# Other landing counts and other drawn due times for a planner that orders one core's instructions at build time

## The chip, the cores and the metric

The kernel runs on one core of one Trainium2 chip. Its time is the device time of one execution in microseconds (us); the median of several executions counts. A core has a tensor engine (PE, with its weight loads shown apart as PEld), a vector engine (DVE), a scalar engine (ACT), a general engine (POOL) and a queue engine (SP). Each runs its own list of instructions strictly in the order in which it was written, and waits on semaphores where an instruction needs another engine's result or a landed transfer. Transfers (DMAs) are issued from SP and POOL here. A DMA issued from POOL can add to what lies at its destination.

## The reference

```python
def _attn_ref(q, k, v, g_norm):                   # q, k, v: (8, 8, 576, 64) float32
    kv = np.einsum('bhsd,bhse->bhde', k, v)
    out = np.einsum('bhsd,bhde->bhse', q, kv)
    rms = np.sqrt(np.mean(out * out, axis=-1, keepdims=True) + 1e-06)
    return out / rms * g_norm

def _moe_ref(x, domain_probs, w1, w2):            # x: (4608, 512); 4 experts, 512 -> 1024 -> 512
    p = domain_probs / (domain_probs.sum(-1, keepdims=True) + 1e-09)
    for e in range(4):
        h = np.maximum(x @ w1[e], 0.0)
        out += p[:, e:e + 1] * (h @ w2[e])
```

The first function's output, with heads beside each other, is the second one's x. All is float32.

## The kernel before

**Tiles and stages.** The 4608 rows of x are worked on in 9 chunks of 512 (eight batches, and one chunk of what is left over of each). There are 36 steps, one for each expert and chunk: steps 0 to 8 are expert 0, and so on. Attention for the next chunk runs beside the steps of expert 0; its results are written to HBM and loaded again for experts 1 to 3. At the end of an expert (steps 8, 17 and 26) the next expert's weights are loaded.

**Products.** The matrix products use a Strassen-Winograd scheme, in parts in two levels: seven products in place of eight, of sums and differences of blocks. PE multiplies; ACT and DVE copy and add PE's results out of its banks; DVE and POOL form the sums and differences (L549), either engine where the planner gives it a choice. Each product is issued by `halves_of` (L526) as matmuls on half the array; one product of the inner level is eight of them.

**Weights.** For experts 1 to 3 a difference that needs a block of weights from HBM is made by `subtract_from`: ACT copies a tile with its sign changed (L622), then POOL issues a DMA that adds the HBM block onto it (L628): an *adding weight transfer*. Plain weight loads go through `load` on SP (L555).

**Output.** A chunk's output is collected in `big` buffers. Expert 0 writes it out plainly on SP (L1592); experts 1 to 3 add it onto what lies in HBM, by DMAs from POOL (L1590): *adding output writes*. The very last chunk loads what is there, adds and writes plainly.

**The order.** Nothing is ordered at run time. The program first lists all operations (`plan.add`), each with a key (its place in the sequence of steps), the engines that may run it with a cost on each, the buffers that it reads and writes, and for a DMA its size and `lands`, the least time counted from issue to landing. `Plan.prepare` gives each operation a due time (`base`): from the PE work ahead of its key, pulled forward along its dependences. `Plan.run` then plays the program through: each time that an engine is free, it takes among the operations that are ready the one with the earliest due time (SP takes the first ready one by key), gives it a buffer slot, and writes down the order. `Plan.begin` sets when a DMA's result counts as landed. The instructions are then emitted in that order. So a different landing count or due time moves no work; it changes which operation stands before which, which of DVE and POOL runs a sum, and which buffer slot a result gets.

**Drawn due times.** `Plan.layout` goes step by step. For each step, `deal` looks up a number in the table DEALS and shifts the due times of the operations of that step and the next by noise drawn from that number (`noise`, a hash, the same in each build), with one of three widths for PE operations and one of three others for the rest. A step without an entry has no noise.

Of the kernel before, what the change touches and what calls it, by code (L numbers as in the profile page):

```python
# [41 lines left out]
class Plan:  # L42
# [18 lines left out]
    FORMS = 9.0  # L61
    STEP, LATE = 44.0, 30.0
    SLOW = 6.8
    SPREADS = 1.0, 2.0, 4.0
    SPREADS_PE = 0.0, 0.5, 1.5
    RATE, RATE_POOL, OPEN = 260.0, 130.0, 36.0
    FIRST = "SP",
    DEALS = {
        -2: 8, -1: 32, 0: 171, 1: 147, 2: 82, 3: 196, 4: 105, 5: 75, 6: 79, 7: 39, 8: 54, 9: 73, 10: 115,
        11: 84, 12: 12, 13: 6, 14: 6, 16: 1, 17: 3, 18: 10, 19: 11, 20: 2, 21: 1, 22: 4, 23: 4, 25: 5, 26:  # L70
        8, 27: 6, 33: 3, 34: 4
    }
    SHARED, AHEAD, INORDER = ("big",), 0.3, ("xf",)

# [90 lines left out]
            self.steps.setdefault(math.floor(op.key), []).append(op)  # L165

    @staticmethod
    def noise(*key):

        def mix(x):  # L170
            x = (x ^ x >> 16) * 0x7feb352d & 0xffffffff
            x = (x ^ x >> 15) * 0x846ca68b & 0xffffffff
            return x ^ x >> 16

        n, step, i = key
        x = mix(n * 2654435761 + (step + 8) * 40503 & 0xffffffff)
        x = mix(x + i * 2246822519 & 0xffffffff)
        y = mix(x + 1 & 0xffffffff)
        total = float(x & 0xffff) + float(x >> 16) + float(y & 0xffff) + float(y >> 16)
        return total / 65536.0 * 1.7320508 - 3.4641016  # L180

    def deal(self, step, n):

        k = len(self.SPREADS)
        wide = self.SPREADS[n % k] if n else 0.0
        wide_pe = self.SPREADS_PE[n // k % len(self.SPREADS_PE)] if n else 0.0
        for op in self.steps[step] + self.steps.get(step + 1, []):
            z = wide_pe if "PE" in op.cost else wide
            op.due = op.base + (z * self.noise(n, step, op.n) if z else 0.0)

    def layout(self, *how):

        self.prepare(*how)
        for step in sorted(self.steps):
            self.deal(step, self.DEALS.get(step, 0))
            assert self.run(step + 1)
        self.run(math.inf)
        assert not self.left
        self.length = max(o.end for o in self.order)
        return self.order  # L200
# [130 lines left out]
    def begin(self, op, eng):  # L331
        t, wake, free = self.t, self.wake, self.free
        op.start, op.eng = t, eng
        if eng == "SP":
            self.busy[eng] = t + op.cost[eng]
            self.bus = max(self.bus, t + 1.5) + op.kb / (215.0 if t < self.OPEN else self.RATE)
            op.end = self.bus + 0.5
            if t >= self.OPEN:
                op.end = max(op.end, t + op.lands)
            self.lanes = self.lanes[1:] + [op.end]  # L340
        else:
            op.end = t + op.cost[eng]
            self.busy[eng] = op.end - (self.OVERLAP[eng] if t >= self.OPEN else 0.0)
            if op.kb:
                self.bus_pool = max(self.bus_pool, op.end + 2.0) + op.kb / self.RATE_POOL
                op.end = max(op.end + op.lands, self.bus_pool)
        if eng == "PE":
            self.worked += op.cost[eng]
        if op.port:
            self.port, self.held = op.end, eng  # L350
            heapq.heappush(wake, op.end + self.TURN["DVE"])
            heapq.heappush(wake, op.end + self.TURN["POOL"])
            heapq.heappush(wake, op.end)
        for b in op.outs:
            if b.kind is not None and b.slot is None:
                free[b.kind].sort()
                b.slot = free[b.kind].pop(next(
                    (i for i, f in enumerate(free[b.kind])
                     if self.written.get((b.kind, f[1]), 0) >= op.wants), 0) if op.wants else 0)[1]
                b.ap = self.slots[b.kind][b.slot]  # L360
        if eng == "PE":
            for b in op.outs:
                self.written[b.kind, b.slot] = op.wide.get(b, op.marks[1] if op.marks else 0)
        for held in list(self.waiting.values()) + list(self.first.values()):
            held.pop(op, None)
        for o in self.after[op]:
            self.missing[o] -= 1
            if not self.missing[o]:
                self.arm(o)
        for b in op.bufs:  # L370
            b.left -= 1
            if b.left == 0 and b.kind is not None:
                early = t < self.OPEN
                end = max(
                    o.end + (0.2 if early else self.AFTER_PE if o.eng == "PE" else self.FREED)
                    for o in [op] + b.readers + b.writers)
                free[b.kind].append((end, b.slot))
                self.live[b.kind] -= 1
                self.ended[b.kind] = max(end, self.ended.get(b.kind, 0.0))
                for rule in [r for r in self.later if not any(self.live.get(k) for k in r[0])]:  # L380
                    self.later.remove(rule)
                    end = max(self.ended[k] for k in rule[0])
                    for ap in rule[2]:
                        free.setdefault(rule[1], []).append((end, len(self.slots[rule[1]])))
                        self.slots[rule[1]].append(ap)
                    heapq.heappush(wake, end)
        heapq.heappush(wake, self.busy[eng])
        if t < self.OPEN:
            heapq.heappush(wake, op.end + 0.06)
            heapq.heappush(wake, op.end + 0.2)  # L390
        if op.kb:
            heapq.heappush(wake, op.end + self.LANDED)
        else:
            for more in (0.0, self.AFTER_PE) if eng == "PE" else (
                    self.SAME, self.TO_PE, self.TO_POOL, self.OTHER):
                heapq.heappush(wake, op.end + more)
        self.order.append(op)
        self.left -= 1
# [3 lines left out]
def kernel(  # L402
# [147 lines left out]
            reads=reads, writes=writes, port=True, after=after,  # L550
        )

    def load(key, buf, dst, src, kb, reads=(), also=(), lands=4.0, issue=0.55):
        plan.add(
            key, {"SP": issue}, lambda eng: nc.sync.dma_start(out=dst(), in_=src), reads=reads,  # L555
            parts=[buf] + list(also), kb=kb, lands=lands,
        )
# [52 lines left out]
    def w1_src(e, dh, uh):  # L610
        rows = moe_w1[e][dh * 2 * P:(dh + 1) * 2 * P, uh * HF:(uh + 1) * HF]
        return rows.rearrange("(kt p) f -> p kt f", p=P)

    def w2_src(e, uh, dh):
        rows = moe_w2[e][uh * HF:(uh + 1) * HF, dh * HN:(dh + 1) * HN]
        return rows.rearrange("(kt p) d -> p kt d", p=P)

    def subtract_from(key, to, view, a, src, reads, writes):

        plan.add(  # L620
            key, act(2 * NT),
            lambda eng: nc.scalar.activation(  # L622
                out=to.ap[:], in_=a.ap[:], func=ACT.Copy, scale=-1.0),
            reads=reads, writes=[to],
        )
        plan.add(
            key, {"POOL": 1.3},
            lambda eng: nc.gpsimd.dma_start(out=view(to.ap), in_=src, accum_op=ALU.add),  # L628
            reads=[to], writes=writes, kb=512, lands=6.0,
        )  # L630

    def weights_1(e, key, step, need):

        f = {n: Buf("big", f"w1_{e}_{n}") for n in (1, 2, 21, 4, 5, 6, 7, 3)}
        corner = {}
        w1corner[e] = {}
        for i, (n, dh, uh) in enumerate(((1, 0, 0), (2, 1, 0), (21, 0, 1), (4, 1, 1))):
            corner[n] = Buf(None, f"w1c_{e}_{n}")
            w1corner[e][uh, dh] = f[n], corner[n]
            load(  # L640
                key + i * step if e or i else -2.75, f[n],
                lambda n=n: f[n].ap[:].rearrange("p (k u) -> p k u", k=2),
                w1_src(e, dh, uh), 512 if e else 300, also=[corner[n]], lands=6.0,
            )

        def form(k_, o, a, b, op):
# [45 lines left out]
    def weights_2(e, key, step, deep):  # L692

        f = {n: Buf("big", f"w2_{e}_{n}") for n in (1, 12, 2, 3, 5, 6, 7, 4)}
        corner = w2corner[e] = {}
        for i, (n, uh, dh) in enumerate(((1, 0, 0), (2, 1, 0), (12, 0, 1), (3, 1, 1))):
            corner[n] = Buf(None, f"w2c_{e}_{n}")
            load(
                key + i * step, f[n],
                lambda n=n: f[n].ap[:].rearrange("p (k d) -> p k d", k=4),  # L700
                w2_src(e, uh, dh), 512 if e else 330, also=[corner[n]], lands=6.0,
            )

        def form(k_, o, a, b, op):
# [816 lines left out]
    def result(s, e, c, base):  # L1521
# [60 lines left out]
        def send(key, i):  # L1582
# [4 lines left out]
            def fn(eng):  # L1587
# [6 lines left out]
            plan.add(  # L1594
                key, {"POOL": 1.0 * len(where)} if e and not again else {"SP": 0.55 * len(where)},
                fn, reads=[part[i, 0], part[i, 1]] + ([was] if was else []), writes=[now], kb=256,
                lands=5.6 if e and not again else 4.5,
                holds=[acc[i // 2]],
            )

# [309 lines left out]
    with tc.manual_schedule(engines={ENG.PE, ENG.DVE, ENG.Activation, ENG.Pool, ENG.SP}):  # L1910
# [7 lines left out]
        wide = {}  # L1918
# [42 lines left out]
```

## Time and profile before

| | us |
|---|---|
| median of 3 executions | 1648.17 |
| lowest, highest | 1646.45, 1650.07 |
| the profiled execution's own time | 1651.69 |
| its span, first to last instruction | 1649.9 |
| PE busy in it | 1632.6 |
| DVE busy | 1316.6 |
| ACT busy | 972.8 |
| POOL busy | 620.5 |

The trace comes from one execution, the profiled one. In the rows below, `L526` is line 526 of the kernel above; `u`, `db` and `ab` are PE's banks, `big`, `xf`, `small`, `snap`, `w1y`, `w2y` and `kv` are tiles in the core's memory, `in_moe_w_dram` are the weights in HBM and `out_dram` the output. A chain of waits is read from its end back: each row is what the next one had waited for. SPq is SP issuing a transfer, and a row "DMA a<-b" lasts from its issue to its landing. In a view by windows the columns are the window, its length, then for each engine the busy time and the number of instructions, then the granted clock of PE as a share of the full one, the DMA engines' busy share and GB/s.

### The profile page before, as it was taken

What the parts mean: (1) busy time and instruction counts of PE and PEld (TensorE: products, weight loads), DVE (VectorE), ACT (ScalarE), POOL (GpSimd) and SP (SyncE); (2) the same over time, 40 slices, a digit from 0 to 9 for tenths busy, and PEclk for the clock granted to TensorE, in tenths of its full rate; (3) what the DMA queues carried; (4) which work ended last, traced back from release to release, by engine and by line L of the source; (5) the groups of instructions that cost most, each with busy time, mean ns of one, the idle gap of its engine ahead of it and who ended that gap; (6) DMA issues with size and microseconds to landing.
All of it is one profiled execution on the core that took longest, in us unless ns stands there. A gap on an engine that the chain in (4) does not pass through costs nothing.

```text
span 1649.9 us, 66218 instructions
## 1 busy us (share of the span) xinstructions
PE 1632.6 (99%) x28724; PEld 1554.8 (94%) x28724; DVE 1316.6 (80%) x2188; ACT 972.8 (59%) x2462; POOL 620.5 (38%) x641
## 2 busy tenths in 40 slices
PE   9999999999999999999999999999999999999998
PEld 6688789888999999999999999999999999999997
DVE  5777887878888878788887898777898887778776
ACT  3455554655656666666656666655666566666653
POOL 4132323232433453443344443333344444442333
PEclk9999999999999999999999999999999999999999
DMA  9977886654764435444566444444578444444432
GB/s 230 215 172 206 228 227 174 152 194 175 219 170 130 117 92 155 117 112 109 168 158 167 115 106 119 114 117 113 135 186 187 117 117 117 107 115 116 117 104 53
DMA packets 225597, 240.97 MB, mean 146 GB/s; under 512 B 100890, under 2 KB 165274, under 8 KB 225306
## 3 DMA queue, kind: packets, MB, share of 16 engines
q1 hardware_dynamic: 201690, 199.96, 40.0%
q0 software_dynamic: 23616, 36.78, 14.8%
q8 instruction: 225, 3.69, 0.9%
q14 instruction: 66, 0.54, 0.1%
HBM read 162.21 MB, written 74.47 MB: 143 GB/s over the span
## 4 chain that ended last, share of the span: by engine, by line
PE 92%; DMA 4%; SPq 2%; DVE 1%; issue 1%; ACT 0%; POOL 0%; DVEq 0%; POOLq 0%; ACTq 0%
PE u L526 45%; PE db L526 29%; PE ab L526 15%; DMA out_dram<-big 1%; SPq L555 1%; PE ab L1077 1%; DMA big<-in_moe_w_dram 1%; DMA kv<-in_v_dram 1%; PE ab L1102 1%; DVE big L549 0%; PE ab L1144 0%; DMA big<-roots 0%; PE db L1102 0%; PE ab L1906 0%; PE u L890 0%
## 5 line engine op out<-in xcount | busy, mean ns | idle before, releaser
L549 DVE TENSOR_TENSOR big<-big,big 128x1024 f32<-128x1024 f32 (+1 forms) x539 | 502.0, 946 | 44.8 <-ACT big L1381 18.0
L526 PE MATMUL u<-xf,big 128*64 128x128 f32 x6496 | 476.0, 273 | 0.3
L526 PE MATMUL db<-big,big 128*64 128x128 f32 (+1 forms) x5552 | 425.7, 290 | 1.5 <-ACT big L1745 0.9
L526 PE MATMUL u<-xf,w1y 128*64 128x128 f32 x5304 | 396.5, 273 | 3.8 <-ACT u L1417 2.4
L526 PEld LDWEIGHTS u<-xf,big 128*64 128x64 f32 x6496 | 382.4, 137 | 5.1 <-ACT snap L1417 1.4
L526 PEld LDWEIGHTS db<-big,big 128*64 128x64 f32 x5552 | 332.1, 137 | 28.9 <-ACT big L1745 1.4
L526 PEld LDWEIGHTS u<-xf,w1y 128*64 128x64 f32 x5304 | 314.1, 137 | 8.1 <-ACT u L1417 2.6
L1425 DVE TENSOR_TENSOR big<-u,snap 128x256 f32<-128x256 f32 x448 | 188.3, 421 | 121.2 <-PE u L526 83.7
L1417 ACT ACTIVATE snap<-u 128x256 f32<-128x256 f32 x490 | 187.9, 384 | 148.7 <-PE u L526 130.3
L549 POOL TENSOR_TENSOR big<-big,big 128x256 f32<-128x256 f32 (+1 forms) x145 | 152.7, 1055 | 219.2 <-DVE big L549 111.3
L1417 ACT ACTIVATE big<-u 128x256 f32<-128x256 f32 x448 | 171.1, 385 | 86.9 <-PE u L526 68.0
L549 POOL TENSOR_TENSOR big<-big 128x512 f32<-128x512 f32 (+1 forms) x89 | 107.3, 1207 | 250.7 <-DVE big L549 115.6
L1745 ACT ACTIVATE snap<-db 128x256 f32<-128x256 f32 (+1 forms) x256 | 90.4, 353 | 122.8 <-PE db L526 100.7
L1381 ACT ACTIVATE big<-big 128x1024 f32<-128x1024 f32 x127 | 133.7, 1054 | 12.3 <-DVE big L549 11.2
L1753 DVE TENSOR_TENSOR big<-ab,snap 128x256 f32<-128x256 f32 x174 | 73.2, 421 | 64.4 <-ACT snap L1745 42.6
L1590 POOL DMA_DIRECT2D out_dram<-big x122 | 106.7, 1233 | 31.9 <-ACT big L1566 24.2
L1417 ACT ACTIVATE u<-u 128x256 f32<-128x256 f32 x245 | 90.8, 371 | 37.6 <-PE u L526 25.1
L549 DVE TENSOR_TENSOR big<-big 128x512 f32<-128x512 f32 (+1 forms) x145 | 109.0, 755 | 1.6 <-ACT big L1381 1.5
L526 PE MATMUL ab<-kv,big 128*64 128x128 f32 x1416 | 99.6, 273 | 0.0
L1566 ACT ACTIVATE big<-big,p_all 128x256 f32<-128x256 f32 x200 | 94.1, 503 | 1.6 <-POOL big L1784 0.7
L526 PE MATMUL ab<-big,big 128*64 128x128 f32 (+1 forms) x1304 | 91.3, 274 | 0.0
L1784 POOL TENSOR_TENSOR big<-big 128x512 f32<-128x512 f32 x25 | 31.9, 1274 | 145.1 <-DVE big L549 125.3
(216 smaller groups left out, 2325.5 us busy)
## 6 DMA issues: line engine op xcount, KB each, us to landing
xf<-x SPq DMA_DIRECT2D x104, 512.0 KB, 3.6
xf<-x_h SPq DMA_DIRECT2D x85, 256.0 KB, 3.1
xf<-x SPq DMA_DIRECT2D x78, 256.0 KB, 3.4
out_dram<-big POOLq DMA_DIRECT2D x74, 256.0 KB, 6.5
x<-xf SPq DMA_DIRECT2D x36, 512.0 KB, 5.0
big<-in_moe_w_dram SPq DMA_DIRECT2D x31, 512.0 KB, 5.7
x_h<-big SPq DMA_DIRECT2D x18, 512.0 KB, 4.6
out_dram<-big SPq DMA_DIRECT2D x32, 256.0 KB, 2.8
```

The costliest lines, as they stand in the source:

```text
L526: nc.tensor.matmul(out_[cols], lhsT=lhsT[:, cols], rhs=rhs, **kw)
L549: lambda eng: adder(eng).tensor_tensor(out=out_(), in0=a(), in1=b(), op=op),
L555: key, {"SP": issue}, lambda eng: nc.sync.dma_start(out=dst(), in_=src), reads=reads,
L1077: nc.tensor.matmul(bank.ap[o * D:(o + 1) * D, r * D:(r + 1) * D], lhsT=ks[r], rhs=vs[r], start=(j == r == 0), stop=(j == len(sets[0]) - 1) ...
L1381: lambda eng: nc.scalar.activation(out=b.ap[:], in_=b.ap[:], func=ACT.Relu),
L1417: lambda eng: nc.scalar.activation(out=where(), in_=ps.ap[:, 0:HN], func=ACT.Copy),
L1425: lambda eng: nc.vector.tensor_tensor(out=block(whole, a, t), in0=src.ap[:, 0:HN], in1=add_.ap[:], op=ALU.add),
L1566: lambda eng: nc.scalar.activation(out=cell(i, half), in_=ap(), func=ACT.Copy, scale=prob()),
L1590: nc.gpsimd.dma_start(out=dst, in_=cell(i)[parts, :], accum_op=ALU.add)
L1745: lambda eng: nc.scalar.activation(out=where(), in_=group_of(ps.ap), func=ACT.Copy),
L1753: lambda eng: nc.vector.tensor_tensor(out=cell(tq, dq), in0=group_of(src.ap), in1=group_of(add_.ap), op=ALU.add,),
L1784: lambda eng: adder(eng).tensor_tensor(out=whole(to), in0=whole(a), in1=whole(b), op=ALU.add),
```

## The change

Three things are changed in the planner and its inputs; no operation is added or taken away.

1. Counted landings: weight loads 6.0 to 6.7 us, adding weight transfers 6.0 to 8.2, adding output writes 5.6 to 6.3, the default of `load` 4.0 to 4.6. A factor MARGIN on these counts is brought in and stands at 1.0.
2. Due times: a step now has a list of draws in place of one. For each draw an operation gets noise of that draw's width only if a second hash falls below the draw's share (all, a fifth or a twentieth of the operations), and the noises are summed.
3. The table DEALS: other numbers, chosen anew, with one to five draws a step, and entries for steps that had none. They were chosen by playing the order through with drawn landing times; that search is not part of the program.

```diff
-    SPREADS = 1.0, 2.0, 4.0
-    SPREADS_PE = 0.0, 0.5, 1.5
-    RATE, RATE_POOL, OPEN = 260.0, 130.0, 36.0
+    SPREADS, SPREADS_PE, SHARES = (1.0, 2.0, 4.0), (0.0, 0.5, 1.5), (1.0, 0.2, 0.05)
+    RATE, RATE_POOL, OPEN, MARGIN = 260.0, 130.0, 36.0, 1.0
     FIRST = "SP",
     DEALS = {
-        -2: 8, -1: 32, 0: 171, 1: 147, 2: 82, 3: 196, 4: 105, 5: 75, 6: 79, 7: 39, 8: 54, 9: 73, 10: 115,
...
+        -2: (1,), -1: (13, 338, 664), 0: (188, 403, 587, 914), 1: (206, 471, 512, 1170), 2: (239, 316, 726,
+        990, 1105), 3: (141, 481, 724, 916, 1063), 4: (149, 369, 719, 834, 1102), 5: (232, 373, 674, 885,
...
     }
+    def draw(self, n, step, i):
+        x = self.mix(n * 2654435761 + (step + 8) * 40503 & 0xffffffff)
+        return self.mix(x + i * 2246822519 & 0xffffffff)
+
+    def chosen(self, n, step, i):
+        return self.mix(self.draw(n, step, i) + 7 & 0xffffffff) / 4294967296.0
...
-    def deal(self, step, n):
-
-        k = len(self.SPREADS)
-        wide = self.SPREADS[n % k] if n else 0.0
-        wide_pe = self.SPREADS_PE[n // k % len(self.SPREADS_PE)] if n else 0.0
+    def deal(self, step, draws):
+
+        k, kp = len(self.SPREADS), len(self.SPREADS_PE)
         for op in self.steps[step] + self.steps.get(step + 1, []):
-            z = wide_pe if "PE" in op.cost else wide
-            op.due = op.base + (z * self.noise(n, step, op.n) if z else 0.0)
+            op.due = op.base
+            for n in draws:
+                spread = self.SPREADS_PE[n // k % kp] if "PE" in op.cost else self.SPREADS[n % k]
+                share = self.SHARES[n // (k * kp) % len(self.SHARES)]
+                if spread and self.chosen(n, step, op.n) < share:
+                    op.due += spread * self.noise(n, step, op.n)
...
-            self.deal(step, self.DEALS.get(step, 0))
+            self.deal(step, self.DEALS.get(step, ()))
...
-                op.end = max(op.end, t + op.lands)
+                op.end = max(op.end, t + op.lands * self.MARGIN)
...
-                op.end = max(op.end + op.lands, self.bus_pool)
+                op.end = max(op.end + op.lands * self.MARGIN, self.bus_pool)
...
-    def load(key, buf, dst, src, kb, reads=(), also=(), lands=4.0, issue=0.55):
+    def load(key, buf, dst, src, kb, reads=(), also=(), lands=4.6, issue=0.55):
...
-            reads=[to], writes=writes, kb=512, lands=6.0,
+            reads=[to], writes=writes, kb=512, lands=8.2,
...
-                w1_src(e, dh, uh), 512 if e else 300, also=[corner[n]], lands=6.0,
+                w1_src(e, dh, uh), 512 if e else 300, also=[corner[n]], lands=6.7,
...
-                w2_src(e, uh, dh), 512 if e else 330, also=[corner[n]], lands=6.0,
+                w2_src(e, uh, dh), 512 if e else 330, also=[corner[n]], lands=6.7,
...
-                lands=5.6 if e and not again else 4.5,
+                lands=6.3 if e and not again else 4.5,
```

More of the change, by code (lines that the diff above doesn't have):

```diff
@@ L63 @@
     SLOW = 6.8
-    SPREADS = 1.0, 2.0, 4.0
-    SPREADS_PE = 0.0, 0.5, 1.5
-    RATE, RATE_POOL, OPEN = 260.0, 130.0, 36.0
+    SPREADS, SPREADS_PE, SHARES = (1.0, 2.0, 4.0), (0.0, 0.5, 1.5), (1.0, 0.2, 0.05)
+    RATE, RATE_POOL, OPEN, MARGIN = 260.0, 130.0, 36.0, 1.0
     FIRST = "SP",
     DEALS = {
-        -2: 8, -1: 32, 0: 171, 1: 147, 2: 82, 3: 196, 4: 105, 5: 75, 6: 79, 7: 39, 8: 54, 9: 73, 10: 115,
-        11: 84, 12: 12, 13: 6, 14: 6, 16: 1, 17: 3, 18: 10, 19: 11, 20: 2, 21: 1, 22: 4, 23: 4, 25: 5, 26:
-        8, 27: 6, 33: 3, 34: 4
[6 rows of a table added]
     }
@@ L167, in noise, with mix @@
     @staticmethod
[L168 to L178, printed above, removed]
+    def mix(x):
+        x = (x ^ x >> 16) * 0x7feb352d & 0xffffffff
+        x = (x ^ x >> 15) * 0x846ca68b & 0xffffffff
+        return x ^ x >> 16
+    def draw(self, n, step, i):
[3 more added lines that the diff above has]
+        return self.mix(self.draw(n, step, i) + 7 & 0xffffffff) / 4294967296.0
+    def noise(self, n, step, i):
+        x = self.draw(n, step, i)
+        y = self.mix(x + 1 & 0xffffffff)
         total = float(x & 0xffff) + float(x >> 16) + float(y & 0xffff) + float(y >> 16)
         return total / 65536.0 * 1.7320508 - 3.4641016
-    def deal(self, step, n):
-        k = len(self.SPREADS)
-        wide = self.SPREADS[n % k] if n else 0.0
-        wide_pe = self.SPREADS_PE[n // k % len(self.SPREADS_PE)] if n else 0.0
+    def deal(self, step, draws):
+        k, kp = len(self.SPREADS), len(self.SPREADS_PE)
         for op in self.steps[step] + self.steps.get(step + 1, []):
-            z = wide_pe if "PE" in op.cost else wide
-            op.due = op.base + (z * self.noise(n, step, op.n) if z else 0.0)
+            op.due = op.base
[4 more added lines that the diff above has]
+                    op.due += spread * self.noise(n, step, op.n)
     def layout(self, *how):
```

4 rows, old and new, of the table DEALS are left out of this document.

## The prediction

> **What bounds the kernel now.** I read the page's first two parts, then what the tensor engine (PE) waits for, the busy time by windows, and the chain of waits around each place where PE stood still.
>
> ```profile
> span 1649.9 us, 66218 instructions
> PE 1632.6 (99%) x28724; PEld 1554.8 (94%) x28724; DVE 1316.6 (80%) x2188; ACT 972.8 (59%) x2462; POOL 620.5 (38%) x641
> PEclk9999999999999999999999999999999999999999
> ```
>
> PE works for 1632.6 of 1649.9 us; the vector engine (DVE) is idle for 333 us. A new order moves neither matmuls nor bytes, so it can only win back time in which PE stands still or runs below its pace. The windows say where that is.
>
> ```profile
> 80.00:140.00 60.00, 56.91 (x935) 48.78 (x933) 44.91 (x82) 31.97 (x81) 20.27 (x22) 1.00 0.77 194
> 140.00:200.00 60.00, 58.57 (x986) 48.93 (x984) 43.52 (x74) 34.46 (x89) 16.29 (x17) 1.00 0.81 229
> 470.00:500.00 30.00, 27.61 (x476) 27.36 (x474) 23.94 (x41) 19.77 (x47) 12.18 (x14) 0.94 0.80 205
> 850.00:890.00 40.00, 36.86 (x658) 35.55 (x656) 31.13 (x58) 24.28 (x60) 17.89 (x19) 1.00 0.81 183
> 1000.00:1200.00 200.00, 200.00 (x3667) 199.86 (x3664) 158.62 (x235) 122.46 (x314) 67.03 (x67) 1.00 0.44 117
> 1200.00:1400.00 200.00, 200.00 (x3670) 199.96 (x3666) 172.58 (x283) 127.76 (x318) 89.42 (x89) 1.00 0.58 143
> ```
>
> The columns are PE, its weight loads, DVE, ACT and POOL, each with its instructions, then clock, DMA share and GB/s. From 1000 to 1400 us PE is dense: 200 us over 3667 matmuls is 54.5 ns for each, eight of them (one product) 0.44 us. At that pace the window 470 to 500 would hold 550 matmuls and holds 476: 74 x 54.5 ns = 4.0 us lost, of which 2.4 us is idle. The window 850 to 890 would hold 734 and holds 658: 4.1 us lost. The two early windows hold mixed shapes, so only their idle time is read off: 3.1 and 1.4 us.
>
> ```profile
> PE u L526 <- DVE big L1425: 2.9, 4, 1.7
> PE u L526 <- ACT u L1417: 2.4, 1, 2.4
> PE u L526 <- ACT snap L1417: 2.2, 1, 2.2
> PE u L526 <- DVE small L1425: 0.9, 1, 0.9
> ```
>
> The waits agree: the 2.4 us is the stop near 488, the 2.2 and 0.9 us are those near 881 and 864, and most of the first row lies before 200 us. ACT and DVE are named, but the chain shows what they had waited for. First stop:
>
> ```profile
> 475.32 1.33 PE u L526 x24
> 476.65 10.09 DMA out_dram<-big
> 486.82 0.04 ACT big L622
> 487.78 0.37 ACT u L1417
> 488.20 1.97 PE u L526 x16
> ```
>
> An output write (chunk 7 of expert 0, on SP) took 10.09 us. The sign-flip copy of L622 reuses its buffer and waits for it, and the small copy that seeds PE's next product stands behind that on ACT. Second stop:
>
> ```profile
> 853.33 8.19 DMA out_dram<-big
> 861.64 1.24 DVE big L549
> 863.99 1.33 DVE big L549
> 865.45 0.73 POOL big L549
> 868.74 11.33 DMA big<-in_moe_w_dram
> 881.05 0.37 ACT snap L1417
> 881.47 0.66 PE u L526 x8
> ```
>
> An adding output write took 8.19 us, a DVE sum and what follows it came late, and then an adding weight transfer took 11.33 us while ACT's next sign-flip stood waiting for it.
>
> After the first stop there is a second loss:
>
> ```profile
> 486.00:488.20 2.20, 0.00 (x1) 0.00 (x1) 0.61 (x2) 1.38 (x3) 0.03 (x1) 0.98 1.12 289
> 488.20:491.20 3.00, 3.00 (x28) 3.00 (x30) 0.95 (x2) 2.12 (x5) 2.02 (x2) 0.50 0.47 93
> ```
>
> For 3.0 us the granted clock is 0.50 and 28 matmuls run where 55 would: 1.5 us more. So a stop of 2.4 us costs 4.0 us, and avoiding it wins all of that. The Trainium skill ("TensorE: Matmul & The Clock Gate", Part 1: The HAM clock gate) has the clock halved only after an idle window of about 3.4 us, by which this stop would cost its 2.4 us alone and the sum below would be -7.5 us. The rows show the halved clock after 2.4 us, and the measurement decides.
>
> **The change part by part.** The counted landings go up in the planner: weight loads 6.0 to 6.7 us, adding weight transfers 6.0 to 8.2, adding output writes 5.6 to 6.3, other loads 4.0 to 4.6. That itself emits nothing; MARGIN is 1.0 and multiplies nothing. The traced medians:
>
> ```profile
> out_dram<-big POOLq DMA_DIRECT2D x74, 256.0 KB, 6.5
> big<-in_moe_w_dram SPq DMA_DIRECT2D x31, 512.0 KB, 5.7
> out_dram<-big SPq DMA_DIRECT2D x32, 256.0 KB, 2.8
> big<-in_moe_w_dram POOLq DMA_DIRECT2D x16, 512.0 KB, 8.6
> x_h<-big SPq DMA_DIRECT2D x18, 512.0 KB, 4.6
> ```
>
> The old count of an adding weight transfer, with its 1.3 us of issue, was 7.3 us against 8.6 traced; the new one is 9.5. The plain output write keeps its count. The Trainium skill ("DMA: Bandwidth & Descriptors", Anatomy of one DMA) gives 2.0 us plus bytes over 436 GB/s, an estimate of 3.2 us for 512 KB; by that the old counts were ample, the longer ones would win nothing at the second stop, and the sum would be -6.0. The row of 8.6 us says otherwise.
>
> The draws decide which of several ready operations goes first. The instruction orders of the two programs hold the same 2778 PE operations (12 fillers among them), the same 706 SP operations with all their DMAs, and 18 element-wise sums more on DVE and 18 fewer on POOL.
>
> ```profile
> L549 DVE TENSOR_TENSOR big<-big,big 128x1024 f32<-128x1024 f32 (+1 forms) x539 | 502.0, 946 | 44.8 <-ACT big L1381 18.0
> ```
>
> 18 x 0.95 us = 17 us at most, inside DVE's 333 us of idle: nothing. If it had no cover, the bound is 17 us.
>
> What the new order does to lateness I read as *cover*: the matmul work, at 0.44 us a product, that stands in PE's order between the last matmul that must end before a transfer can be issued and the first that cannot start before it has landed, through buffers and queues alike. A transfer whose landing and follow-up exceed its cover stops PE.
>
> *First stop.* The late write had a cover of 10.5 us and landed after 10.09, too long once ACT's two copies follow. In the new order its buffer goes to a POOL sum much later: cover 20.1 us. The adding weight transfers beside it go from 13.5 and 11.8 to 15.7 us each. Next late is then the copy's other source, the adding transfer issued before it:
>
> ```profile
> 474.22 1.30 POOL L628 DMA_DIRECT2D big<-in_moe_w_dram  x1 [0.41 <-ACT big L622]
> ```
>
> With the median of 8.6 us it lands at 482.8, 4 us before the copy began. I take all 4.0 us back; bounds 0 (that transfer late in its place) and -4.0.
>
> *Second stop.* The output write goes from 10.5 to 13.5 us, the adding weight transfer from 12.2 to 15.3. The 3.1 us more come out of the 4.1 lost: -3.1; bounds 0 and -4.1.
>
> *Before 200 us.* The idle time is 4.5 us there. The longest wait, 1.7 us at 83, hangs on loads of q whose cover is 14.2 us in both orders: it stays. The broadcast loads of the roots of batch 2 go from 10.0 to 14.3 and 10.4 to 19.0 us, the later q loads from 15.5 to 16.4, 16.8 to 20.7 and 13.3 to 15.9. So 2.8 us of idle is in reach, a little more with the refill after each stop: I take -3.0; bounds 0 and -4.5.
>
> *What pays for it.* Some covers shrink: plain writes of chunk 0's output 22.4 to 9.0, of chunk 2's 12.0 to 9.8, of chunk 6's 14.8 to 10.9, a copy of x 25.9 to 11.2, one weight load 13.1 to 10.5. Their kinds land in 2.8, 4.6 and 5.7 us by the medians above, so they hold unless one lands like the write at 476.65. Waits between DVE, ACT and PE in the new order appear in no row of before; the nearest are the 0.9 us rows. I take +1.0 for all of these; bounds 0 and +4.0, one more stop like the first.
>
> The sum: -4.0 - 3.1 - 3.0 + 1.0 = -9.1. The profiled execution took 1651.69 us (span 1649.9 and 1.8 around it), so 1642.6. That execution lies 3.5 us above the median of the runs, 1648.17. If the 3.5 us are late landings of the kind that the change covers, the new kernel's median is near 1642.6 as well; if they are a constant of profiling, it is 1648.2 - 9.1 = 1639.1. Since the runs themselves spread over 3.6 us, I take the first: 1642.5, and 1636 to 1645 as this case's own range. After the last matmul nothing is won: the last sixteen operations are the same.
>
> **The rivals.**
>
> *The stops were an accident of that execution.* Then other runs (1646.45 the lowest) don't hold them, and only the early part is won: 1648.2 - 3.0 + 1.0 = 1646.2. For it: one plain write of 10.09 us stands against a median of 2.8. Against: the adding transfers' median of 8.6 is no accident. The estimate of 3.2 us above is on this rival's side, and the same row speaks against it.
>
> *The stops move.* The covers grow where the rows show stops, but another transfer is late in the same 30 us, where DMA is busy to 0.80 of its time; the early gain is paid back by the shrunken covers. 1648, between 1645 and 1651.
>
> *Slower: SP's short covers.* The five shrunken covers all hang on SP before 450 us, where its queue is fullest. Each write that lands in 10 us instead of 3 to 6 stops PE past 2.4 us, halves its clock and costs 4.0 us. Keeping the gain (5.6 us on the median, or 6.6 without the +1.0), one is 1645.6, two 1649.6, three 1653.6: it turns slower at the third. For it: their covers are now 9.0 to 11.2 us, like the 10.5 us that failed. Against: only one plain write was that late in before's 1650 us.
>
> **How the numbers follow.** The forecast gets 0.54, the accident 0.14, moved stops 0.14, SP's short covers 0.18. 0.2% (3.3 us, what a measurement of this kernel can tell) puts faster below 1644.9 and slower above 1651.5. The forecast's case is faster, two rivals are the same, the last slower: 0.54, 0.28, 0.18. The range reaches down to 1635.5 (the lower case, 1639.1, less the 3.6 us over which the runs spread) and up to 1652, which takes in the two same cases and the mild end of the slower one; some 0.05 is left out below and 0.14 above.
>
> **What would show it.** Right: from 450 to 900 us PE is dense at 54.5 ns, no granted clock of 0.50 after the start, ACT's sign-flips of L622 (L631 in the new lines) wait for no DMA, and the windows before 200 us hold under 2.5 us of idle. Wrong: a PE stop of 2 us or more whose chain goes through an output write on SP before 450 us, or through an adding transfer that outlasted 13 to 16 us.

## The result and the profile after

The changed kernel takes 1640.43 us, the median of 6 executions (1638.08 to 1642.09), beside 1649.12 us for the kernel before in its 6 (1646.45 to 1651.61). The ratio is 0.9946, its 95% interval 0.9932 to 0.9960: 8.7 us faster. The forecast was faster, 1642.5 us.

Two rows of the changed kernel's page (its line numbers are nine higher here: L526 is now L535):

```profile
span 1636.3 us, 66175 instructions
PE 1627.5 (99%) x28724; PEld 1554.3 (95%) x28724; DVE 1309.6 (80%) x2206; ACT 970.9 (59%) x2462; POOL 627.5 (38%) x623
```

The same 28724 matmuls stand in a span that is 13.6 us shorter. Most of that came out of stops. PE's own waits, in full:

```profile
PE ab L1915 <- POOL ident masks.py:199: 1.4, 1, 1.4
PE ab L958 <- DVE big L833: 1.2, 1, 1.2
PE u L535 <- DVE big L1434: 1.0, 1, 1.0
PE db L535 <- ACT ab L1754: 1.0, 1, 1.0
```

The waits behind L1417 (now L1426), 2.4 and 2.2 us before, are gone. Of the four that are left, the first two lie in the opening. The windows of the prediction, in the changed kernel:

```profile
80.00:140.00 60.00, 58.97 (x998) 50.93 (x996) 45.21 (x82) 36.02 (x94) 20.41 (x21) 1.00 0.79 200
140.00:200.00 60.00, 59.94 (x1006) 51.49 (x1002) 42.95 (x78) 32.97 (x84) 18.73 (x18) 1.00 0.80 220
470.00:500.00 30.00, 30.00 (x555) 30.00 (x552) 27.77 (x46) 20.75 (x50) 12.24 (x13) 1.00 0.83 193
850.00:890.00 40.00, 39.05 (x717) 38.81 (x714) 34.21 (x59) 24.19 (x60) 19.01 (x20) 1.00 0.76 177
```

The window 470 to 500 is dense: 555 matmuls where there were 476, at 54.5 ns each 4.3 us won. The window 850 to 890 has 717 for 658, 3.2 us won, 0.9 us of idle left. The early idle time is 1.0 + 0.1 us for 3.1 + 1.4: 3.4 us won. But the early part won more than its idle time. At 400 us attention's matmuls have ended in both kernels (the last at 348 and 340 us), and what is left are products, dense at 54.5 ns a matmul, so the count of matmuls done by then says how far each has come. First before, then the changed kernel:

```profile
0.00:400.00 400.00, 392.66 (x6204) 322.15 (x6206) 297.38 (x551) 210.94 (x535) 121.41 (x148) 1.00 0.75 200
0.00:400.00 400.00, 396.13 (x6309) 328.75 (x6311) 294.44 (x566) 214.04 (x544) 136.84 (x143) 1.00 0.75 201
```

The changed kernel is 105 matmuls ahead, 5.7 us, of which 3.5 us were idle before. With 4.3 and 3.2 us these make 13.2 of the 13.6 us. Through the first stop's place the chain of waits now runs on PE alone:

```profile
485.34 0.44 PE u L535 x8
485.78 0.87 PE ab L535 x16
486.65 1.31 PE u L535 x24
487.96 0.87 PE db L535 x16
```

The medians from issue to landing of the transfers in question are

```profile
out_dram<-big POOLq DMA_DIRECT2D x76, 256.0 KB, 6.4
big<-in_moe_w_dram SPq DMA_DIRECT2D x31, 512.0 KB, 6.3
big<-in_moe_w_dram POOLq DMA_DIRECT2D x17, 512.0 KB, 6.9
out_dram<-big SPq DMA_DIRECT2D x32, 256.0 KB, 4.2
```

An adding weight transfer has 6.9 us where it had 8.6, a plain weight load 6.3 for 5.7. Neither difference repeats: in a second profile of each kernel the first has 7.6 us for 7.7 before, the second 6.4 for 6.5. Only the plain output writes are later in both, 4.2 and 3.9 us for 2.8 and 2.8.

### The profile page after: what moved, and what is told of

It reads as the page before. It is cut to its first block, busy times and chain, and to the rows that moved or that the text cites. A ratio compares the mean times of both kernels' runs of the same rounds, so it can differ in the third digit from the quotient of the medians.

```text
span 1636.3 us, 66175 instructions
## 1 busy us (share of the span) xinstructions
PE 1627.5 (99%) x28724; PEld 1554.3 (95%) x28724; DVE 1309.6 (80%) x2206; ACT 970.9 (59%) x2462; POOL 627.5 (38%) x623
## 4 chain that ended last, share of the span: by engine, by line
PE 97%; DMA 1%; SPq 1%; DVE 0%; ACT 0%; issue 0%; POOL 0%; DVEq 0%; POOLq 0%; ACTq 0%
PE u L535 47%; PE db L535 31%; PE ab L535 15%; PE ab L1086 1%; PE ab L1111 1%; PE ab L1153 0%; PE db L1111 0%; SPq L564 0%; DMA x<-small 0%; DMA snap<-roots 0%; PE ab L1915 0%; PE u L899 0%; DMA small<-in_q_dram 0%; PE db L938 0%; PE ab L958 0%
## 5 line engine op out<-in xcount | busy, mean ns | idle before, releaser
L535 PE MATMUL u<-xf,big 128*64 128x128 f32 x6784 | 495.6, 273 | 0.1
L558 DVE TENSOR_TENSOR big<-big,big 128x256 f32<-128x256 f32 (+1 forms) x512 | 463.1, 920 | 33.7 <-ACT big L1390 10.3
L535 PE MATMUL db<-big,big 128*64 128x128 f32 (+1 forms) x5632 | 434.1, 290 | 0.0
L535 PEld LDWEIGHTS u<-xf,big 128*64 128x64 f32 x6784 | 399.6, 137 | 4.0 <-issue 1.5
L535 PE MATMUL u<-xf,w1y 128*64 128x128 f32 x5304 | 394.0, 273 | 0.0
L535 PEld LDWEIGHTS db<-big,big 128*64 128x64 f32 x5632 | 339.2, 137 | 26.2 <-ACT small L1035 0.3
L535 PEld LDWEIGHTS u<-xf,w1y 128*64 128x64 f32 x5304 | 314.4, 137 | 3.3 <-DVE xf L558 0.8
L1426 ACT ACTIVATE snap<-u 128x256 f32<-128x256 f32 x490 | 187.2, 383 | 154.7 <-PE u L535 129.7
L558 POOL TENSOR_TENSOR big<-big,big 128x256 f32<-128x256 f32 (+1 forms) x157 | 184.9, 1180 | 227.7 <-DVE big L558 102.0
L1426 ACT ACTIVATE big<-u 128x256 f32<-128x256 f32 x444 | 169.2, 383 | 76.6 <-PE u L535 55.1
L558 POOL TENSOR_TENSOR big<-big 128x512 f32<-128x512 f32 (+1 forms) x82 | 101.6, 1240 | 211.8 <-DVE big L558 125.7
L1426 ACT ACTIVATE u<-u 128x256 f32<-128x256 f32 x245 | 90.7, 370 | 49.2 <-PE u L535 39.2
L535 PE MATMUL ab<-kv,big 128*64 128x128 f32 x1528 | 105.9, 273 | 0.0
L535 PE MATMUL ab<-big,big 128*64 128x128 f32 (+1 forms) x1288 | 92.1, 275 | 0.0
L1575 ACT ACTIVATE big<-big,p_all 128x256 f32<-128x256 f32 x192 | 89.3, 501 | 3.6 <-DVE big L1793 2.2
L535 PEld LDWEIGHTS ab<-kv,big 128*64 128x64 f32 x1528 | 89.0, 137 | 0.0
```

What stands on the lines that cost most here:

```text
L535: nc.tensor.matmul(out_[cols], lhsT=lhsT[:, cols], rhs=rhs, **kw)
L558: lambda eng: adder(eng).tensor_tensor(out=out_(), in0=a(), in1=b(), op=op),
L1426: lambda eng: nc.scalar.activation(out=where(), in_=ps.ap[:, 0:HN], func=ACT.Copy),
L1575: lambda eng: nc.scalar.activation(out=cell(i, half), in_=ap(), func=ACT.Copy, scale=prob()),
```

## The experiments

The theory: late adding transfers, and a plain write, outlast the matmul work that covers them; longer counts put more work there, and the new draws win the early part. Its rivals: the stops were an accident of one execution, the draws do it all, or the stops only move. "Lost" below is a window's missing matmuls times 54.5 ns; a dense window of 30 us holds 550, of 40 us 734, of 100 us 1834.

### The kernel before once more

No edit.

> The kernel before, unchanged, profiled once more. Cover theory: PE stops again near 488 and near 864 to 881, and the windows 470 to 500 and 850 to 890 lose 2 us or more each against the dense pace. Rival, the two stops were an accident of one execution: both windows lose under 1 us.

1650.36 us, one execution. Two windows of it, then its chain:

```profile
470.00:500.00 30.00, 28.49 (x519) 28.01 (x517) 26.05 (x45) 21.47 (x51) 12.61 (x15) 1.00 0.89 212
850.00:890.00 40.00, 36.02 (x644) 34.77 (x640) 30.07 (x57) 23.52 (x57) 16.80 (x17) 1.00 0.76 169
```

```profile
475.85 9.03 DMA out_dram<-big
...
850.92 8.64 DMA out_dram<-big
...
866.78 11.67 DMA big<-in_moe_w_dram
```

Both stops are back: 31 matmuls (1.7 us) and 90 (4.9 us) are missing, against 4.0 and 4.1 us in the first profile. The first falls short of the 2 us that were expected. Its write takes 9.03 us where it took 10.09, PE stands still for 1.3 us where it was 2.4, and the clock is not halved. At the second stop the same write takes 8.64 us (8.19 before), the same weight transfer 11.67 (11.33). That repeats to 0.5 us: how long these two take belongs to their place in the order. The first stop has a place too, but its size varies.

### The counts alone, and the draws alone

The counts alone, in the kernel before:

```diff
-... load(..., lands=4.0, ...)            # other loads
+... load(..., lands=4.6, ...)
-... kb=512, lands=6.0,                   # adding weight transfers
+... kb=512, lands=8.2,
-... also=[corner[n]], lands=6.0,         # weight loads, twice
+... also=[corner[n]], lands=6.7,
-lands=5.6 if e and not again else 4.5,   # output writes
+lands=6.3 if e and not again else 4.5,
```

> The kernel before with the new counted landings alone, its old draws kept. Cover theory: nothing changes before 400 us; the second stop's covers go from 10.5 to 17.5 and from 12.2 to 14.8 us and it is gone, the first's from 10.5 to 12.7 and from 11.8 to 13.5 and it loses half or more: 4 to 7 us faster than before, 1642 to 1645. Rival, the draws make the gain and the counts nothing: 1648 to 1650.

1642.37 us, ratio 0.9959 (0.9947 to 0.9971): 6.8 us faster than the kernel before beside it (1649.16).

```profile
470.00:500.00 30.00, 29.18 (x532) 28.75 (x530) 24.84 (x43) 21.35 (x50) 13.91 (x14) 1.00 0.85 206
850.00:890.00 40.00, 40.00 (x738) 40.00 (x735) 35.89 (x59) 27.16 (x67) 24.22 (x20) 1.00 0.91 187
```

The second stop is gone altogether, the first loses 1.0 us. Five numbers, with draws that were chosen for other numbers, bring most of the gain. "The draws make the gain and the counts nothing" falls.

The reverse, the changed kernel with the five counts set back (and two of step 7's five draws left out):

> The changed kernel's draws with the old counts (the two draws of step 7 left out). Cover theory: loads of k and v for batches 3 and 4 now have a cover of 4.6 us, under their traced median of 4.7 to 5.0, and an adding weight transfer has 10.9: more than 5 us lost again before 200 us and a stop near 480, 1648 to 1660. Rival, the draws make the gain whatever the counts: 1639 to 1642.

1674.78 us, ratio 1.0151 (1.0136 to 1.0166), slower than even the theory's range. Two windows, and two of PE's waits over the whole span:

```profile
0.00:400.00 400.00, 378.98 (x5812) 306.32 (x5814) 278.53 (x514) 201.51 (x502) 103.21 (x127) 0.99 0.68 180
200.00:400.00 200.00, 188.36 (x3032) 162.05 (x3034) 142.66 (x246) 107.01 (x265) 46.60 (x53) 0.99 0.60 167
```

```profile
PE db L528 <- ACT small L1028: 5.9, 6, 2.0
PE ab L1146 <- ACT big L1128: 2.1, 2, 1.2
```

11.6 us of idle lie between 200 and 400 us, where the kernel before has 0.4. The reason that was given is wrong, though: no wait for k or v is among them. For 6.9 of the 11.6 us PE waits for ACT, which copies attention's results out of the banks (L1028, 4.8 us there) and squares them (L1128, 2.1 us). The stage is lost mostly in the hand-offs between PE and ACT, not at loads with 4.6 us of cover. The stop that was expected near 480 us didn't come: 533 matmuls from 470 to 500 us, 0.9 us lost.

### No draws at all

`DEALS = {}` in the kernel before, and in the changed kernel.

> The kernel before without any draws, old counts. Cover theory: loads of k and v with covers of 4.6 us stop PE in each attention stage, and the late covers (8.7 to 11.8 us) are as short as before's: 1655 to 1680. Rival, the draws matter little: 1646 to 1652.

1675.78 us, ratio 1.0153 (1.0139 to 1.0167).

> The changed kernel without any draws, new counts. Cover theory: the same 4.6 us covers early, so as slow there as without draws on the old counts; the adding weight transfers' covers are 14.0 to 16.2 in place of 11.4 to 13.5 us, so 1 to 5 us faster than the old counts without draws. Rival, the counts are the gain by themselves: 1640 to 1645.

1672.46 us, ratio 1.0133 (1.0117 to 1.0148). Both are about as slow as the new draws on the old counts (1674.78): those draws lose all their worth under counts for which they weren't chosen. That is no rule, for the old draws kept theirs under the new counts (1642.37 us against 1672.46 without draws). Between the two kernels without draws the counts win 3.3 us. One reading speaks against the cover as a sufficient sign. Without draws on the old counts, the second stop's write and transfer have covers of 12.2 and 11.8 us, where the kernel before has 10.5 and 12.2; the transfer's is shorter than before, yet there is no stop:

```profile
850.00:890.00 40.00, 40.00 (x738) 40.00 (x736) 37.77 (x62) 25.65 (x66) 18.52 (x18) 1.00 0.73 175
890.00:930.00 40.00, 40.00 (x738) 40.00 (x734) 36.88 (x64) 25.59 (x61) 19.88 (x19) 1.00 0.71 162
```

(This program runs some 25 us later.) A short cover is a place that can stop. What decides whether it does wasn't tried; that it hangs on what else lands at that time is a guess.

### Early part and late part apart

The changed planner with the old draws in one of its halves, cut at expert 0's step 7; old draws apply to all operations (share 1). Of the counts, expert 0's weight loads go with the early half and all others with the late one, the default of `load` too, throughout the program.

```diff
-                share = self.SHARES[n // (k * kp) % len(self.SHARES)]
+                share = 1.0 if step in self.WHOLE else self.SHARES[n // (k * kp) % len(self.SHARES)]
```

> The order of before up to expert 0's seventh step, the new counts and draws from there. Cover theory: the time lost before 200 us stays at before's 8 to 9 us; of the two late stops the second shrinks as in the changed kernel (its covers are the same, 13.5 and 15.3 us), the first keeps an output write with a cover of 10.0 us but its adding weight transfers have 14.8 and 15.7: 3 to 7 us faster than before, 1642 to 1646. Rival, the gain is all in the early part: 1648 to 1650. Rival, the stops were an accident of one execution: 1648 to 1650, too.

1644.91 us, ratio 0.9979 (0.9969 to 0.9988): 4.2 us faster.

```profile
80.00:140.00 60.00, 57.11 (x921) 49.48 (x918) 42.01 (x76) 31.02 (x78) 19.91 (x21) 0.97 0.76 186
470.00:500.00 30.00, 30.00 (x552) 29.89 (x550) 24.15 (x45) 22.46 (x52) 15.66 (x14) 1.00 0.72 189
850.00:890.00 40.00, 38.55 (x708) 38.30 (x705) 34.67 (x59) 26.79 (x63) 20.25 (x21) 1.00 0.81 180
```

The early idle is as before (2.9 us in this window), the first stop is gone, the second loses 1.4 us: 1.5 us of idle near 863, with ACT's sign-flip waiting 2.0 us for a plain weight load.

> The changed kernel's order up to expert 0's seventh step, the old counts and draws from there. Cover theory: under 4 us lost before 200 us, and both late stops as in before (covers 10.5 and 12.2 us at the second, 8.7 to 11.4 at the first): 4 to 6 us faster than before, 1643 to 1645. Rival, the late stops were all of the gain: 1648 to 1650. Rival, the stops were an accident: all of the gain is early, 1640 to 1642.

1647.26 us, ratio 0.9986 (0.9978 to 0.9995): 1.9 us faster, less than expected.

```profile
0.00:400.00 400.00, 395.85 (x6309) 328.57 (x6311) 294.01 (x566) 214.40 (x544) 136.54 (x142) 1.00 0.75 201
850.00:890.00 40.00, 35.30 (x600) 34.11 (x598) 27.68 (x50) 22.48 (x55) 15.07 (x15) 0.96 0.66 156
```

The early part wins in full: 6309 matmuls by 400 us, as many as the changed kernel. But the second stop loses 134 matmuls, 7.3 us, where the kernel before loses 4.1 and 4.9. So part of an early gain was given back at a stop further on. Early and late add up to 6.1 of the change's 8.7 us.

Before step 7 this kernel differs from the one with all counts set back in one number, expert 0's weight loads (6.7 us against 6.0), and the other did 5812 matmuls by 400 us. So 0.7 us in a single count decides whether these draws fit.

### One late write

The kernel before, with expert 0's last output writes counted long:

```diff
-lands=5.6 if e and not again else 4.5,
+lands=5.6 if e and not again else 10.1 if s == 7 else 4.5,
```

> The kernel before with one edit: expert 0's output writes of chunk 7 count 10.1 us in place of 4.5. Cover theory: up to 470 us and at the second stop all stays as it was (covers 10.5 and 12.2 us); at the first stop the writes' covers go from 10.5 to 14.0 us or more and that of the adding weight transfer from 11.8 to 12.7, and the stop is gone: 3 to 4 us faster than before, 1645 to 1646. Rival, the stop moves to the next late transfer: 1648 to 1650.

1649.72 us, ratio 0.9996 (0.9985 to 1.0007): nothing. Three windows of it, then the middle one in the kernel before:

```profile
470.00:500.00 30.00, 30.00 (x554) 30.00 (x552) 26.50 (x44) 22.43 (x54) 14.91 (x15) 1.00 0.92 217
500.00:600.00 100.00, 98.87 (x1792) 97.35 (x1788) 86.51 (x138) 59.97 (x158) 49.31 (x44) 1.00 0.41 112
850.00:890.00 40.00, 37.26 (x666) 36.02 (x664) 31.54 (x58) 23.91 (x58) 16.48 (x17) 1.00 0.76 171
```

```profile
500.00:600.00 100.00, 100.00 (x1836) 99.95 (x1834) 82.69 (x141) 61.48 (x159) 43.07 (x42) 1.00 0.41 112
```

The stop is gone, as the theory has it. But what follows is another order, for which the old draws weren't chosen: 44 matmuls, 2.4 us, are lost between 500 and 600 us, where the kernel before loses none; an adding output write of 7.30 us stands in the chain there. Here the rival is right: the stop moved.

### Which count removes the second stop

The kernel before with the adding weight transfers' count alone, and with all the others:

> The kernel before with one count changed: adding weight transfers 8.2 us in place of 6.0. Its matmul order is before's up to the first stop. If the late adding output write starts the second stop, that stop stays (the write's cover is 10.5 us as before, the transfer's 13.1 against 12.2): 2 us or more lost from 850 to 890, and 1 to 3 us faster in all by the first stop, 1647 to 1649. Rival, the adding weight transfer alone makes the second stop: under 1 us lost there, 1643 to 1645.

1647.62 us, ratio 0.9984 (0.9975 to 0.9993).

> The kernel before with the other new counts and adding weight transfers at the old 6.0 us. Its matmul order is before's up to 600 us, so the first stop stays. If the late adding output write starts the second stop, that stop is gone or under 1.5 us (the write's cover is 17.5 us in place of 10.5, the transfer's 11.8 against 12.2): 3 us faster than before, 1645 to 1647. Rival, the adding weight transfer alone makes it: 3 us or more lost there, 1648 to 1650.

1646.58 us, ratio 0.9975 (0.9963 to 0.9987). The window 850 to 890, first of the one with the weight transfers' count, then of the other:

```profile
850.00:890.00 40.00, 37.13 (x667) 36.10 (x665) 32.03 (x60) 23.93 (x59) 16.25 (x18) 1.00 0.76 171
```

```profile
850.00:890.00 40.00, 38.69 (x706) 38.21 (x704) 33.21 (x53) 26.82 (x63) 24.49 (x19) 1.00 0.89 186
```

With the weight transfers' count alone 67 matmuls (3.7 us) stay lost; its chain still has the late write and the late transfer:

```profile
850.78 8.56 DMA out_dram<-big
...
866.55 11.44 DMA big<-in_moe_w_dram
```

With the other counts 28 (1.5 us) stay lost. This fits what the chain said: the late output write starts the second stop, and the weight transfer behind it makes the rest. The output writes' count was not tried without the loads' counts, so that it is the writes' is argued and not shown. It takes both halves to lose nothing there. Against 1650.42 us the two win 2.8 and 3.8 us, together 6.6: what the five counts win at once.

### Mixed, and the changed kernel once more

The changed kernel's draws up to step 6, the old draws from there, the new counts throughout: the best halves of both, if they add up.

> The changed kernel's draws up to expert 0's seventh step, before's draws from there, the new counts throughout. If the parts add up, it loses before 200 us what the changed kernel loses (3 to 4 us) and after 400 us what the new counts with the old draws lose (2 to 3 us): 1639 to 1641, level with the changed kernel or a little faster. Rival, the parts depend on each other: output writes of chunk 7 with a cover of 8.7 us and a load of x with 6.1 us stop PE again, 1643 or more.

1641.56 us, ratio 0.9949 (0.9937 to 0.9961), just over what was expected.

```profile
500.00:600.00 100.00, 99.47 (x1798) 97.58 (x1794) 83.51 (x140) 58.67 (x154) 46.80 (x41) 1.00 0.41 109
850.00:890.00 40.00, 39.76 (x727) 39.39 (x724) 35.41 (x59) 26.86 (x65) 22.55 (x20) 1.00 0.87 194
```

It loses almost nothing at the second stop, but 2.1 us between 500 and 600. The changed kernel beside it is 2.7 us faster:

> The changed kernel, unchanged, on the same chip and in the same rounds as the three beside it, profiled once more. Cover theory: 8 to 10 us faster than before, no stop from 470 to 500 us, at most 1.5 us lost from 850 to 890, and 4 us or less before 200 us. Rival, its clean trace was luck: stops of over 1 us in places that the first trace doesn't show.

1638.86 us, ratio 0.9935 (0.9923 to 0.9947): 11.6 us below the kernel before beside it (1650.42), more than expected. There is no stop from 470 to 500 us and 1.2 us of early idle, but the stop near 858 is longer than expected. Two windows and the chain:

```profile
850.00:890.00 40.00, 37.58 (x659) 37.33 (x657) 32.38 (x53) 23.05 (x57) 17.09 (x17) 0.96 0.77 168
859.70:863.00 3.30, 3.30 (x36) 3.30 (x34) 3.30 (x4) 1.39 (x4) 1.47 (x2) 0.50 1.15 251
```

```profile
845.99 11.01 DMA big<-in_moe_w_dram
...
857.98 0.37 ACT big L1426
858.35 0.28 ACT ab L1754
858.63 0.04 issue
858.68 1.10 PE db L535 x16
```

A plain weight load on SP took 11.01 us, ACT's sign-flip (L631) stood waiting for it, and PE behind ACT; PE stood still for 2.4 us, and 1 us after it went on the clock fell to 0.50. In all 75 matmuls are lost, 4.1 us. No kernel of these beats the changed one.

## Why the prediction was right, step by step

*What bounds it.* Right: the gain is in PE's stops, and 0.50 of the clock was part of the first one's price. Not all of it is stops, though: 2.2 us of the early gain show as matmuls that follow each other more closely.

*First stop, -4.0.* The mechanism is right (the write's buffer is no longer needed soon; the window is dense in both profiles of the changed kernel). Profile against profile it is 4.3 us, but the second profile of before lost only 1.7 there, and the kernel with all new counts but the adding weight transfers', whose matmul order is before's up to 600 us, lost 1.2 (528 matmuls). So 4.0 is the upper end of what it is worth.

*Second stop, -3.1.* 3.2 us in the first pair of profiles, 0.8 in the second pair (644 matmuls before, 659 after). The two kernels with one half of the counts fit a chain that the output write leads. What was missed: the changed order has a stop of its own there, behind a plain weight load whose cover went from 14.4 to 11.4 us. The prediction's list of shrunken covers ended at 450 us and didn't hold it. The slower rival's mechanism, a short cover on SP, is thus real. It struck later than that rival put it, in all three profiles that hold this order there: 1.0, 1.5 and 2.4 us of idle. With the slow clock in the last it cost 4.1 us, about what was priced.

*Before 200 us, -3.0.* The place is right and the size is too small: the term was read off idle time alone, 3.4 us by the windows. By the matmuls done up to 400 us the early part is worth 5.7 us, and 4.9 in the second profiles (6220 and 6309). It is no accident: seven profiles with the old draws before step 7 have 6194 to 6240 by then, four with the new ones 6309 to 6318. The q loads' wait stayed, as foretold, 1.7 us before and 1.0 after. Why the rest went was not tried one by one: the covers of the roots' loads did grow, but the kernels without fitting draws show that this stage can also be lost, by far more, in hand-offs between PE and ACT, of which the prediction said nothing.

*What pays for it, +1.0.* None of the five covers listed makes a stop in either profile. The opening's wait grew from 0.5 to 1.2 us, and there is the weight load.

*From the sum to the median.* The sum was 9.1 us and the medians differ by 8.7. That they are so close is partly luck: the pair of profiles on which the sum was built differs by 13.6 us, the first stop was taken at its upper end, and the early term was too small by 1.9 to 2.7 us. What made the forecast too small is the offset: the profiled execution's 3.5 us over the median were taken as late landings that the change would win, which made 9.1 into 5.7. Over six executions that excess was 2.6 us, and the changed kernel's own profiled execution (1638.08) lies below its median, so the two can't be set off like that. The other end that was named, 1639.1, is 1.3 us away, the forecast 2.1.

*Its own signs.* PE is dense from 450 to 900 us but for the stop near 857, and the early windows hold 1.1 us of idle: so far right. ACT's sign-flips do wait for a transfer, 1.5 us in the first profile and 3.0 in the second, and the second has a granted clock of 0.50 there. Neither sign of being wrong appeared: that stop hangs on a plain weight load, which the list didn't name.

*The rivals.* Accident: refuted by the stops' return. Stops move: true of the single long count (1649.72 us), not of the change. "Counts were ample", with the estimate of 3.2 us from the Trainium skill ("DMA: Bandwidth & Descriptors", Anatomy of one DMA): the counts alone won 6.8 us, and the medians here are 8.6 and 6.9 us for 512 KB (7.7 and 7.6 in the second profiles).

What stays open: how much of the early gain hangs on which wait, and why 2.2 of its 5.7 us show as closer matmuls and not as idle time.

## What to carry to other kernels

Where a planner writes an order out, compare each kind of transfer's counted landing with the traced one, in the crowded stretch above all, and correct the counts before searching for better orders: five numbers won 6.8 us here, under draws that were chosen for the old ones. A single count can win little or nothing (the weight transfers' won 2.8 us, the one longer write none), since the order behind it is new and may not fit its draws. Try draws again after a change of a count: one set here kept its worth under other counts, the other lost it all. To see what an order risks, list the work that covers each transfer over the whole program, not only where it stops today.

## What the runs showed of the hardware

How late a transfer lands belonged to its place at the second stop: the same adding write took 8.19, 8.64 and 8.56 us and the weight transfer behind it 11.33, 11.67 and 11.44 in three profiles (the kernel before twice, and with the weight transfers' count alone), far over the medians of 6.5 and 8.6 in the first of them. At the first stop it varied more, 10.09 and 9.03 us.

A stop of 2.4 us was followed by a granted clock of 0.50 in the profile of before, and one of 2.4 us in the second profile of the changed kernel, for some 3.4 us each. The length of the stop doesn't decide it: in the kernel with the new draws late, one of 2.1 us near 82 was followed by 0.50 (the 0.97 of its first window above), while the stops of 2.2 us near 881 and of 2.5 us near 879, in the two profiles of before, left the clock at 1.00. After the last of these:

```profile
880.00:883.40 3.40, 3.40 (x62) 3.21 (x61) 1.11 (x3) 2.74 (x7) 2.96 (x3) 1.00 1.08 167
```

The Trainium skill ("TensorE: Matmul & The Clock Gate", Part 1) puts the limit at an idle window of about 3.4 us; here shorter stops sufficed, not every time.
